# A Fourier-mixing and expert-lookup kernel: two token blocks row by row instead of one, and half of the table comparison moved into the score part

## Chip, cores and metric

The kernel runs on one core of one Trainium2 chip. The metric is the device time of one execution in microseconds (us), median of three runs; lower is better.

## What is computed

The reference, cut to what matters (S = 2048 tokens, D = 512, H = 32 heads, 64 keys per half, 4096 experts):

```
xn  = layernorm(x)
A   = dft_seq_re @ (xn @ dft_hid_re.T) - dft_seq_im @ (xn @ dft_hid_im.T)
q   = xn @ w_q                          # 32 heads, two halves of 128
s1, s2 = q1 @ k1.T, q2 @ k2.T           # 64 scores per half and head
top 2 of each half -> 4 pairs -> the best 2 experts per head, softmax g over them
act = gelu(xn . u[expert])              # 64 chosen rows of u per token
out = x + A + sum(g * act * v[expert])  # 64 chosen rows of v per token
```

## The kernel before, in words

The 2048 tokens are 16 blocks of 128. The work has three parts, one after the other on TensorE (PE).

- **Fourier part.** The input is normalized, folded by the symmetry of the cosine and sine tables, and multiplied; the result goes to `y_d` in device memory.
- **Score part.** A loop over 8 groups of heads (`j`, `NCH` = 8) and 16 token blocks (`i`): `scores` runs 12 matmuls for one block and group (L705), ScalarE (ACT) copies the result out of PSUM (L710), VectorE (DVE) finds the best keys (L713, L717). Around it ACT and GpSimd (POOL) split the query weights (`m_prep`, L158 to L166) and the tables u and v (`fill_uv`, L608 to L610) into pairs of 16-bit parts. `routing` turns the keys into expert numbers and softmax weights.
- **Expert part.** For 15 blocks (`NB = NT - NS`, `NS` = 1) the lookup is done as dense matmuls over all 4096 experts. `u_part` computes all dot products with u (L834) and a gelu on ACT (L837); `g_mm` builds from the expert numbers, with three DVE operations on 16-bit data (L860, L865, L868), the matrices whose product is the weight of each expert (L870); `w_part` multiplies weight and gelu and splits the product (L878, L882, L883); `v_part` multiplies with v (L890); `finish` adds and stores (L909). A loop over `b` runs `v_part` of block b in 8 steps, with `w_part` of the next block among them, and then `u_part` of block b + 2 in 8 steps, with `g_mm` among them.

The last block of tokens (`NS` = 1) does not go through the dense matmuls. `picked` gathers the 64 chosen rows of u and then the 64 of v for each token, one row per token at a time (`gather`, an indirect DMA issued by POOL, L914, 5 buffers `ga`). `dot` multiplies a row of u by the token and sums it on DVE (L943). `gate` does the gelu and the softmax weight of all 64 at once. `gain` scales a row of v on ACT (L954) and adds it to the output on POOL (L955). After each consumed row the next gather is issued. All dots come first, then all sums. These steps are dealt out evenly over "turns": there is one turn after each step of `v_part` (from b = 1) and of `u_part` (from b = 0 on, that is u of block 2), 16 (NB - 2) + 4 = 212 in all. `pick` orders the DVE and ACT instructions of a turn behind the matmuls of that step in the plan from which each engine's fixed instruction order comes (`follow`: an order, not a wait).

The kernel also verifies that its inputs have the symmetry it uses, and that the 16-bit scales fit. `compare(n)`, 64 of them, loads one 128x1024 piece of the cosine and sine tables, sums its first 128 columns (DVE, L989), subtracts or adds mirrored parts (DVE, L995 to L1029; for pieces 8 to 31 and 40 to 63 only L1008 and L1014, and for two in each eight a small extra), and sums what is left (ACT, L1030). `compare_w` does so for four pieces of the hidden table, `fit` sums absolute values on ACT (L1075, L1081). They are dealt out over the expert part by `step`. `verdict` combines the sums near the end. `add_x` loads the Fourier result for a block and adds x to it by a DMA that POOL issues (L903).

DMAs without another name are issued by SyncE (SP) in order. The tile framework gives out buffers and semaphores; each engine runs its instructions in the planned order.

Of the kernel before, what the change touches and what calls it, by code (L numbers as in the profile page):

```python
# [19 lines left out]
P = 128  # L20
# [12 lines left out]
NS = 1  # L33
# [3 lines left out]
def tile_fnet_peer(ctx, tc, x, ca, cb, c5, wt, wf, wr, wq, kt, ut, un, vn, out):  # L37
# [52 lines left out]
    NF = NW + 32 + NCH - 1  # L90
    sums_sb = cst.tile([P, 138 + NF + 3], F32, name="sums")
# [459 lines left out]
    def part_b(safe, stS, stP, stE, xt, u_sb, cmp_p):  # L551
# [146 lines left out]

        def scores(j, i, vals, idx):
# [3 lines left out]
            for kd in range(KD):  # L703
                for l, r in ((0, 0), (0, 1), (1, 0)):
                    nc.tensor.matmul(ps, xt[i][:, l, kd, :], m[:, r, kd, :], start=(n == 0),  # L705
                                     stop=(n == 3 * KD - 1))
                    n += 1
# [12 lines left out]
            return st[:, 512:]  # L720
# [29 lines left out]
        for (which, g), n in zip(fills, slots):  # L750
            todo[n].append(lambda at, w=which, g=g: fill_uv(w, g, at))
            todo[n - (3 if n < 113 else 1)].append(lambda at, w=which, g=g: fill_load(w, g))
        m_stage(1, wq_tile, 0)
        pend = None
        for j in range(NCH):
# [5 lines left out]
            for i in range(NT):  # L761
                spare = scores(j, i, vals, idx)
# [133 lines left out]
        def follow(i, after):  # L896
            tc.add_manual_dep(i, after.ins.name, mybir.DependencyInfo(
                mybir.DependencyClass.NoSync, mybir.DependencyReason.DATA), reason="pace")

# [12 lines left out]
        def gather(table, n, s):  # L912
            t = bp.tile([P, D], F32, tag="ga", name=f"ga{n}_{s}", bufs=5)
            nc.gpsimd.indirect_dma_start(  # L914
                out=t, out_offset=None, in_=table,
                in_offset=bass.IndirectOffsetOnAxis(ap=eix[:, n].rearrange("p k h -> p (k h)")[:, s:s + 1], axis=0))
            return t

        def picked(n):

            b = NB + n
            N = 2 * H
            G = {}
            T = {}

            def fetch(s):
                if s < 2 * N:
                    G[s] = gather((un, vr)[s // N], n, s % N)

            def begin():  # L930
                xs = T["x"] = bp.tile([P, D], F32, tag="xs", name=f"xs_{n}", bufs=1)
                o = T["o"] = bp.tile([P, D], F32, tag="ov", name=f"ov{n}", bufs=1)
                T["z"] = bp.tile([P, N], F32, tag="za", name=f"za{n}", bufs=1)
                nc.sync.dma_start(xs, x[b // 4, b % 4])
                nc.sync.dma_start(o, y_d[b])
                nc.gpsimd.dma_start(o, x[b // 4, b % 4], accum_op=ALU.add)
                for s in range(AHEAD):
                    fetch(s)
                norm(xs, xs, b)

            def dot(s):
                t = G.pop(s)
                nc.vector.scalar_tensor_tensor(t, t, 1.0, T["x"], op0=ALU.mult, op1=ALU.mult,  # L943
                                               accum_out=T["z"][:, s:s + 1])
                fetch(s + AHEAD)

            def gate():
                za = T["z"]
                nc.scalar.activation(za, za, AF.Gelu_apprx_tanh)
                nc.gpsimd.tensor_tensor(za, za, gts[:, n].rearrange("p k h -> p (k h)"), op=ALU.mult)  # L950

            def gain(s):
                t = G.pop(N + s)
                nc.scalar.activation(t, t, AF.Copy, scale=T["z"][:, s:s + 1])  # L954
                nc.gpsimd.tensor_tensor(T["o"], T["o"], t, op=ALU.add)  # L955
                fetch(N + s + AHEAD)

            return [begin, *(lambda s=s: dot(s) for s in range(N)), gate, *(lambda s=s: gain(s) for s in range(N)),
                    lambda: nc.sync.dma_start(out[b * P:(b + 1) * P], T["o"])]

        vr = vn.rearrange("c p d -> (c p) d")
        picks = [] if safe else [f for n in range(NS) for f in picked(n)]
        more = [range(1, 1 + max(0, n - k * (NB - 2) - 4)) for n, k in ((68, 5), (NF - NCH + 1, 4))]
# [13 lines left out]

        later = []

        def compare(n):  # L980

            ri, g, kk = n // 32, n // 8 % 4, n % 8
            odd = kk // 4
            t = bp.tile([P, 4, 4, 64], F32, tag="w", name=f"cx{n}", bufs=WB)
            tf = t.rearrange("p s q c -> p (s q c)")
            tv = t.rearrange("p s q c -> p s (q c)")
            nc.sync.dma_start(tf[:, :P], ca[ri, g, :, kk * P:(kk + 1) * P])
            nc.sync.dma_start(tf[:, P:], cb[ri, g, kk].rearrange("p b c -> p (b c)"))
            nc.vector.tensor_reduce(asum[:, n:n + 1], tf[:, :P], axis=AX.X, op=ALU.add,  # L989
                                    apply_absolute_value=True)  # L990
            sgn = (((1, 1, 1), (-1, 1, -1)), ((-1, -1, 1), (1, -1, -1)))[ri][odd]
            ops = [ALU.subtract if v > 0 else ALU.add for v in sgn]
# [131 lines left out]
        def step(it):  # L1124
            ready = later[:]
            del later[:]
            for f in ready:
                f()
# [209 lines left out]
```

## Time and profile before

| | |
|---|---|
| median of 3 runs | 1169.99 us (1169.89 to 1170.13) |
| profiled execution, its own time | 1171.21 us |
| profiled execution, span from first to last instruction | 1169.3 us |
| busy share of the span | PE 96%, DVE 84%, ACT 54%, POOL 42% |
| Fourier part, then score part | score matmuls start from 72.3 us to 443.4 us |
| expert part | first dense matmul at 446.6 us, last `v_part` matmul starts at 1162.4 us |
| rows of u gathered | 460.3 to 804.7 us (start of the issue) |
| rows of v gathered, summed | 812.2 to 1123.1 us, last sum starts at 1150.6 us |

In a row of the groups, a line number is followed by the engine, the operation, the tiles written and read, the shape and the count, then the busy time of all in us, the mean of one in ns, and the idle time of the engine just before them with what ended it. In a row of the table by stretches stand, after the stretch and its length, the busy time of each engine with the count of its instructions, the granted clock of PE, the share of the DMA engines and their GB/s. In a row of the timeline stand start and duration in us, engine, line and operation, and in brackets the idle time before it and what ended it.

### The profile page before, as it was taken

How to read it: one execution, taken by the hardware profiler on the slowest of the kernel's cores; microseconds unless marked ns; L12 is line 12 of the kernel's file. 1: busy time of each engine (PE TensorE's matmuls, PEld its weight loads, DVE VectorE, ACT ScalarE, POOL GpSimd, SP SyncE). 2: the span in 40 equal slices, each digit the busy share in tenths (PEclk: the TensorE clock that was granted, in tenths of full speed). 3: DMA queues.
4: the chain of work that ended last, by engine and by line, in shares of the span. 5: the costliest groups of instructions: out<-in, count | busy, mean ns of one | idle time of the engine just before them, and what ended most of it. 6: DMA issues, size and time to landing. Idle time of an engine off the chain costs nothing.

```text
span 1169.3 us, 29061 instructions
## 1 busy us (share of the span) xinstructions
PE 1118.0 (96%) x11681; PEld 734.0 (63%) x11681; DVE 987.5 (84%) x2946; ACT 632.3 (54%) x995; POOL 488.1 (42%) x411
## 2 busy tenths in 40 slices
PE   5799999999999999979999999999998999989997
PEld 4354555454454448939668578687685876858763
DVE  7878888798898997887998887988899689879895
ACT  2575546767767663443543534534546465464563
POOL 0021525548548342131343222323374666656742
PEclk9899999999999999989999999999999999999999
DMA  8254224132231113223554745645536456364554
GB/s 311 78 211 151 85 79 162 55 108 89 93 110 55 55 62 127 58 80 102 169 179 146 217 143 151 202 138 174 181 104 175 132 162 173 109 192 137 158 148 109
DMA packets 74369, 157.02 MB, mean 134 GB/s; under 512 B 10086, under 2 KB 26989, under 8 KB 74224
## 3 DMA queue, kind: packets, MB, share of 16 engines
q1 hardware_dynamic: 61522, 117.30, 30.1%
q0 software_dynamic: 12544, 37.76, 12.4%
q8 instruction: 93, 1.52, 0.5%
q14 instruction: 52, 0.43, 0.1%
q10 hardware_dynamic: 158, 0.01, 0.0%
HBM read 141.08 MB, written 13.96 MB: 133 GB/s over the span
## 4 chain that ended last, share of the span: by engine, by line
PE 71%; DVE 17%; DMA 4%; ACT 4%; issue 3%; SPq 0%; POOL 0%; DVEq 0%; ACTq 0%; POOLq 0%
PE s L705 27%; PE z L834 22%; PE v L890 14%; DVE L L860 3%; PE g L870 3%; DVE act L883 2%; DMA cx<-in_cb_dram 2%; DVE w L878 2%; ACT act L882 2%; DVE R L865 2%; PE m L144 2%; PE p L366 2%; DVE R L868 1%; DVE cx L1008 1%; DVE cx L997 1%
## 5 line engine op out<-in xcount | busy, mean ns | idle before, releaser
L834 PE MATMUL z<-xb,u 128*128 128x128 f16 x5760 | 335.1, 221 | 15.0 <-ACT act L837 12.6
L705 PE MATMUL s<-m,xq 128*128 128x512 f16 x1536 | 338.9, 379 | 0.0
L834 PEld LDWEIGHTS <-u 128*128 128x128 f16 x5760 | 327.6, 99 | 16.1 <-issue 13.3
L890 PE MATMUL v<-v,act 128*128 128x512 f16 x1440 | 319.7, 380 | 0.0
L705 PEld LDWEIGHTS <-xq 128*128 128x128 f16 x1536 | 148.4, 98 | 171.3 <-issue 0.2
L890 PEld LDWEIGHTS <-act 128*128 128x128 f16 x1440 | 138.2, 98 | 160.5 <-issue 1.9
L860 DVE TENSOR_TENSOR L<-io_lam,cmp 128x2048 f16<-128x2048 f16 x120 | 152.6, 1271 | 62.5 <-PE g L870 52.8
L837 ACT ACTIVATE act<-z,scl 128x512 f32<-128x512 f32 x120 | 81.9, 685 | 197.0 <-PE z L834 196.8
L914 POOL DMA_INDIRECT ga<-in_un_dram,eix x64 | 81.7, 1276 | 219.3 <-DVE ga L943 182.0
L713 DVE MAX8 vals<-ss 128x8 f32<-128x64 f32 x1024 | 152.6, 216 | 19.4 <-ACT ss L710 19.2
L955 POOL TENSOR_TENSOR ov<-ov,ga 128x512 f32<-128x512 f32 x64 | 98.3, 1535 | 114.0 <-ACT ga L954 112.4
L710 ACT ACTIVATE ss<-s,wsc 128x512 f32<-128x512 f32 x112 | 75.5, 680 | 81.8 <-PE s L705 71.7
L882 ACT ACTIVATE act<-w 128x1024 f16<-128x1024 f32 x60 | 79.5, 1351 | 54.5 <-DVE w L878 52.0
L717 DVE FIND_INDEX8 idx<-vals,ss 128x8 uint16<-128x256 f32 x256 | 107.1, 418 | 0.0
L914 POOL DMA_INDIRECT ga<-in_vn_dram,eix x64 | 89.2, 1393 | 34.7 <-DVE ga L943 17.3
L1030 ACT ACTIVATE cx<-cx 128x896 f32<-128x896 f32 x64 | 60.5, 946 | 67.4 <-DVE cx L1014 40.6
L883 DVE TENSOR_TENSOR act<-w,act 128x1024 f16<-128x1024 f32 x60 | 81.8, 1363 | 14.3 <-ACT act L882 14.1
L865 DVE TENSOR_TENSOR R<-io_c,cmp 128x512 f16<-128x512 f16 x120 | 81.5, 679 | 0.0
L878 DVE SCALAR_TENSOR_TENSOR w<-act,scl,g 128x1024 f32<-128x1024 f32 x60 | 75.4, 1276 | 2.2 <-PE g L870 1.8
L870 PEld LDWEIGHTS <-L 128*128 128x128 f16 x1920 | 56.4, 96 | 20.2 <-issue 8.0
L870 PE MATMUL g<-R,L 128*128 128x32 f16 x1920 | 58.6, 176 | 10.2 <-DVE R L868 7.8
L166 POOL TENSOR_TENSOR wq<-wq,wh 128x1024 f16<-128x1024 f32 x26 | 55.5, 2133 | 19.1 <-DMA wq<-in_wq_dram 16.4
(271 smaller groups left out, 1241.0 us busy)
## 6 DMA issues: line engine op xcount, KB each, us to landing
cx<-in_cb_dram SPq DMA_DIRECT2D x64, 448.0 KB, 4.4
wq<-in_wq_dram SPq DMA_DIRECT2D x32, 512.0 KB, 6.5
fit<-in_wq_dram SPq DMA_DIRECT2D x28, 512.0 KB, 5.4
uv<-in_ut_dram SPq DMA_DIRECT2D x16, 512.0 KB, 3.7
uv<-in_vn_dram SPq DMA_DIRECT2D x16, 512.0 KB, 3.7
xq<-in_x_dram SPq DMA_DIRECT2D x8, 512.0 KB
xt_d<-xq SPq DMA_DIRECT2D x16, 256.0 KB, 4.1
cx<-in_ca_dram SPq DMA_DIRECT2D x64, 64.0 KB, 2.5
```

The costliest lines, as they stand in the source:

```text
L705: nc.tensor.matmul(ps, xt[i][:, l, kd, :], m[:, r, kd, :], start=(n == 0), stop=(n == 3 * KD - 1))
L713: nc.vector.max(vals[:, i, w, :, h], s[:, g, :])
L717: nc.vector.max_index(idx[:, i, w].rearrange("p k h -> p (k h)"), vals[:, i, w, 0:2].rearrange("p k h -> p (k h)"), s[:, w * HC:g + 1, :]. ...
L834: mm = nc.tensor.matmul(p[:, cc * P:(cc + 1) * P], ug[:, l, c % 2, kd, :], xb[:, r, kd, :], start=(n == 0), stop=(n == 3 * KD - 1))
L860: nc.vector.tensor_tensor(L.rearrange("p t (l two) -> p t l two", two=2), io_lam.rearrange("p (l two) -> p l two", two=2).unsqueeze(1).to_ ...
L865: nc.vector.tensor_tensor(Rv, io_c.rearrange("p (c two) -> p c two", two=2).unsqueeze(1).to_broadcast([P, 16, NC // 2, 2]), bc(1, NC), op= ...
L870: nc.tensor.matmul(p[:, hf, t * NC:(t + 1) * NC], L[:, t, :], R[:, t, :], start=True, stop=True)
L878: nc.vector.scalar_tensor_tensor(w, act[:, :, ts], fw, p.rearrange("p h (n c) -> p c (h n)", c=NC), op0=ALU.mult, op1=ALU.mult)
L882: nc.scalar.activation(w16[..., 0], w, AF.Copy)
L883: nc.vector.tensor_tensor(w16[..., 1], w, w16[..., 0], op=ALU.subtract)
L890: mm = nc.tensor.matmul(pv, w16[:, c, :, l], vg[:, r, c % 2, :], start=(c == 0 and k == 0), stop=(c == NC - 1 and k == 2))
L914: nc.gpsimd.indirect_dma_start(out=t, out_offset=None, in_=table, in_offset=bass.IndirectOffsetOnAxis(ap=eix[:, n].rearrange("p k h -> p ( ...
```

## The change

`NS` becomes 2: 14 blocks go through the dense matmuls, two go row by row, 128 dots and 128 sums. Dots and sums alternate: the list `rows` takes one row of u and, 16 steps behind it, one row of v, and the gathers are issued in that order, still 5 ahead (`AHEAD`). The gelu and the weight are done for 16 dots at a time (`QG`), on ACT and POOL. There are 16 (14 - 2) + 4 = 196 turns for 256 such steps.

`compare` is moved up and takes 32 of its 64 pieces (`EARLY`: 8 to 23 and 40 to 55) in the score part, three and a quarter score tiles apart from tile 20 on. There its subtractions run on POOL in place of DVE, in a tag `cx` of its own with 2 buffers: the load four tiles ahead, the subtractions ordered behind the matmuls of tile n (`hold`), the sums on ACT two tiles later. For all 64, the sum of the first 128 columns moves from DVE to ACT. The 36 pieces that stay and the `fit` steps are dealt out evenly over the steps of `v_part` of blocks 1 to NB - 1 (`paced`).

```diff
-NS = 1
+NS = 2
...
+    EARLY = [*range(8, 24), *range(40, 56)]
+    early = cst.tile([P, 2, len(EARLY)], F32, name="early")
...
+        def hold(f, after):
+            made = nc.cur_bb.bb.instructions
+            first = len(made)
+            f()
+            for i in made[first:]:
+                if i.engine in (mybir.EngineType.DVE, mybir.EngineType.Activation, mybir.EngineType.Pool):
+                    follow(i, after)
...
+        def compare(n, at=None):
...
+            if at is None:
+                t = bp.tile([P, 4, 4, 64], F32, tag="w", name=f"cx{n}", bufs=WB)
+            else:
+                t = sp.tile([P, 4, 4, 64], F32, tag="cx", name=f"cx{n}", bufs=2)
+            v_eng = nc.vector if at is None else nc.gpsimd
...
-            nc.vector.tensor_reduce(asum[:, n:n + 1], tf[:, :P], axis=AX.X, op=ALU.add,
-                                    apply_absolute_value=True)
...
-                    nc.vector.tensor_tensor(v, v, tv[:, 0:1].to_broadcast([P, len(ix), 256]), op=o)
+                        v_eng.tensor_tensor(v, v, tv[:, 0:1].to_broadcast([P, len(ix), 256]), op=o)
...
+            def judge():
+                k = n if at is None else at
+                a, b = (chk, asum) if at is None else (early[:, 0], early[:, 1])
+                nc.scalar.activation(tf[:, P:], tf[:, P:], AF.Abs, accum_out=a[:, k:k + 1])
+                nc.scalar.activation(tf[:, :P], tf[:, :P], AF.Abs, accum_out=b[:, k:k + 1])
...
+        for k in range(len(EARLY)):
+            n = 20 + k * 13 // 4
+            checks.setdefault(n - 4, []).append(lambda mm, k=k: check_load(k))
+            checks.setdefault(n, []).append(lambda mm, k=k: hold(cx[k][0], mm))
+            checks.setdefault(n + 2, []).append(lambda mm, k=k: hold(cx[k][1], mm))
...
+        def fetch():
+            if rows:
+                k, n, s = rows.pop(0)
+                t = T[k, n, s] = bp.tile([P, D], F32, tag="ga", name=f"ga{k}{n}_{s}", bufs=AHEAD)
+                nc.gpsimd.indirect_dma_start(
+                    out=t, out_offset=None, in_=(un, vr)[k],
+                    in_offset=bass.IndirectOffsetOnAxis(ap=eix[:, n].rearrange("p k h -> p (k h)")[:, s:s + 1], axis=0))
+
+        def dot(n, s):
+            if s == 0:
...
+                T["z", n] = bp.tile([P, N], F32, tag="za", name=f"za{n}", bufs=2)
...
+            t = T.pop((0, n, s))
+            z = T["z", n]
+            nc.vector.scalar_tensor_tensor(t, t, 1.0, T["x"], op0=ALU.mult, op1=ALU.mult, accum_out=z[:, s:s + 1])
+            fetch()
+            if s % QG == QG - 1:
+                q = slice(s + 1 - QG, s + 1)
+                nc.scalar.activation(z[:, q], z[:, q], AF.Gelu_apprx_tanh)
+                nc.gpsimd.tensor_tensor(z[:, q], z[:, q], gts[:, n].rearrange("p k h -> p (k h)")[:, q], op=ALU.mult)
+
+        def gain(n, s):
+            b = NB + n
+            if s == 0:
+                T["o"] = o = bp.tile([P, D], F32, tag="ov", name=f"ov{n}", bufs=1)
+                nc.sync.dma_start(o, y_d[b])
+                nc.gpsimd.dma_start(o, x[b // 4, b % 4], accum_op=ALU.add)
+            o = T["o"]
+            t = T.pop((1, n, s))
+            nc.scalar.activation(t, t, AF.Copy, scale=T["z", n][:, s:s + 1])
+            nc.gpsimd.tensor_tensor(o, o, t, op=ALU.add)
+            fetch()
+            if s == N - 1:
+                nc.sync.dma_start(out[b * P:(b + 1) * P], o)
+
+        slots = [(n, s) for n in range(NS) for s in range(N)]
+        for i in range(len(slots) + QG):
+            rows += [(k, *slots[i - k * QG]) for k in range(2) if 0 <= i - k * QG < len(slots)]
+        picks = [] if safe else [lambda k=k, n=n, s=s: (dot, gain)[k](n, s) for k, n, s in rows]
...
+        todo_n = [n for n in range(68) if n not in EARLY]
+        units = [lambda n=n: (compare if n < 64 else compare_w)(n) for n in todo_n]
+        streams = [[fit_units, 0, 0], [units, 0, 0]]
...
+        def paced(k):
+            st = streams[k]
+            st[1] += 1
+            for f in st[0][st[2]:-(-len(st[0]) * st[1] // (4 * (NB - 2) + 2))]:
+                step(f)
+                st[2] += 1
...
-                if 0 < b < NB - 1 and (cg % 2 == 1 or cg == 6) or b + 1 == NB and cg < 4 or cg == 4 and b in more[0]:
-                    step(units)
-                if b and cg % 2 == 0 and (b + 1 < NB or cg < 4) or b + 1 == NB and cg in (1, 3) or (
-                        cg == 3 and b in more[1]):
-                    step(fit_units)
+                if 0 < b < NB - 1 or b + 1 == NB and cg < 4:
+                    paced(cg % 2)
```

More of the change, by code (lines that the diff above doesn't have):

```diff
@@ L910, in finish @@
             nc.sync.dma_start(out[b * P:(b + 1) * P], y)
[L912 to L919, printed above, removed]
-            b = NB + n
[L922 to L934, printed above, removed]
+        vr = vn.rearrange("c p d -> (c p) d")
@@ L947, in gate @@
[L947 to L959, printed above, removed]
```

146 lines of the change are left out of this document (77 added, 69 removed).

## Prediction

> **What bounds the kernel now.** First comes the table by stretches, to see which engine is full in which part: one stretch inside the score part, one of the expert part while rows of u are gathered and dotted, and one while rows of v are summed.
>
> ```profile
> 200.00:400.00 200.00, 200.00 (x1281) 97.21 (x1280) 178.12 (x954) 138.00 (x199) 113.74 (x106) 1.00 0.25 85
> 560.00:810.00 250.00, 248.34 (x3275) 184.56 (x3274) 215.60 (x419) 117.90 (x180) 76.34 (x59) 1.00 0.56 170
> 860.00:1110.00 250.00, 237.27 (x3132) 179.54 (x3130) 215.58 (x295) 133.57 (x207) 153.17 (x106) 0.98 0.52 152
> ```
>
> The columns after the length are PE, its weight loads, DVE, ACT, POOL. PE is full in the score part and in the dots stage. In the sums stage PE loses 12.7 us of 250, DVE is 86% busy as before, and POOL rises from 31% to 61%. How much a block of tokens takes in each stage is read from the DMA that POOL issues once per block, in its timeline:
>
> ```profile
> 564.78 1.02 POOL L903 DMA_DIRECT2D y<-in_x_dram  x1
> ...
> 791.86 1.01 POOL L903 DMA_DIRECT2D y<-in_x_dram  x1
> ...
> 887.98 1.01 POOL L903 DMA_DIRECT2D y<-in_x_dram  x1
> ...
> 1089.38 1.00 POOL L903 DMA_DIRECT2D y<-in_x_dram  x1
> ```
>
> Five blocks in the dots stage take 227.1 us, 45.4 us each; four in the sums stage take 201.4 us, 50.35 us each. PE does the same work in both. The groups of the two stretches show why the second is longer, first 560 to 810 us:
>
> ```profile
> L834 PE MATMUL z<-xb,u 128*128 128x128 f16 x2051 | 117.5, 219 | 1.4 <-ACT act L837 1.4
> L943 DVE SCALAR_TENSOR_TENSOR ga<-ga,xs 128x512 f32<-128x512 f32 x53 | 36.0, 685 | 0.0
> L865 DVE TENSOR_TENSOR R<-io_c,cmp 128x512 f16<-128x512 f16 x43 | 18.0, 419 | 0.0
> L868 DVE TENSOR_TENSOR R<-R,cmp 128x512 f16<-128x512 f16 x42 | 17.6, 420 | 0.5
> L943 DVE DVE_READ_ACCUMULATOR ga<-ga,xs 128x1 f32 x53 | 4.5, 85 | 0.0
> ```
>
> then 860 to 1110 us:
>
> ```profile
> L834 PE MATMUL z<-xb,u 128*128 128x128 f16 x1969 | 118.0, 224 | 10.6 <-ACT act L837 10.6
> L955 POOL TENSOR_TENSOR ov<-ov,ga 128x512 f32<-128x512 f32 x51 | 76.7, 1503 | 82.4 <-ACT ga L954 81.9
> L865 DVE TENSOR_TENSOR R<-io_c,cmp 128x512 f16<-128x512 f16 x42 | 44.7, 1064 | 0.0
> L1008 DVE TENSOR_TENSOR cx<-cx 128x512 f32<-128x512 f32 (+1 forms) x40 | 26.9, 715 | 3.5 <-DMA cx<-in_cb_dram 3.5
> L1030 ACT ACTIVATE cx<-cx 128x896 f32<-128x896 f32 x25 | 23.6, 946 | 27.9 <-DVE cx L1014 19.3 <-DVE cx L1022 4.1 <-DVE cx L1029 3.6
> L868 DVE TENSOR_TENSOR R<-R,cmp 128x512 f16<-128x512 f16 x42 | 22.1, 526 | 0.6
> L1014 DVE TENSOR_TENSOR cx<-cx 128x128 f32<-128x128 f32 (+2 forms) x30 | 9.3, 323 | 0.2
> L989 DVE TENSOR_REDUCE sums<-cx 128x1 f32<-128x128 f32 x25 | 7.0, 281 | 6.5 <-DMA cx<-in_ca_dram 6.5
> ```
>
> The same operation L865 takes 419 ns beside the gathers and 1064 ns beside POOL's sums, L868 420 and 526 ns. A sum on POOL and these DVE operations hinder each other, and the time for which the dots left DVE is eaten by it.
>
> **The change part by part.** *One block fewer in the dense matmuls.* The stretch in which rows are picked is bounded by these rows of the PE timeline:
>
> ```profile
> 526.83 13.56 PE L834 MATMUL z<-xb,u 128*128 128x128 f16 x240
> ...
> 1131.58 31.24 PE L890 MATMUL v<-v,act 128*128 128x512 f16 x144
> ```
>
> From u of the third block at 526.8 us to the end of the last v at 1162.8 us are 636.0 us: 13 blocks of u and v, and one v part alone (96 of the 144 matmuls, 20.8 us). So a block takes (636.0 - 20.8) / 13 = 47.3 us on the mean. After the change there are 12 such blocks and the v part: 12 P + 20.8 us, with P the time per block. At 47.3 us the kernel would gain 47 us. It breaks even at P = 51.3 us, with the score part's 2 us below at 51.1 us. All hangs on P.
>
> *POOL.* 256 steps over 196 turns are 128 / 196 x 16 = 10.45 pairs per block: a gather of u, a gather of v, a sum. The page has their means:
>
> ```profile
> L955 POOL TENSOR_TENSOR ov<-ov,ga 128x512 f32<-128x512 f32 x64 | 98.3, 1535 | 114.0 <-ACT ga L954 112.4 <-DMA cx<-in_ca_dram 1.1
> L914 POOL DMA_INDIRECT ga<-in_vn_dram,eix x64 | 89.2, 1393 | 34.7 <-DVE ga L943 17.3 <-POOL ov L955 16.0 <-DMA fit<-in_wq_dram 0.8
> L914 POOL DMA_INDIRECT ga<-in_un_dram,eix x64 | 81.7, 1276 | 219.3 <-DVE ga L943 182.0 <-DVE sums L989 15.1 <-PE z L834 9.1
> ```
>
> and its timeline the gaps between them and the two ends of their price:
>
> ```profile
> 463.14 0.95 POOL L914 DMA_INDIRECT ga<-in_un_dram,eix  x1 [0.30 <-issue]
> ...
> 831.26 0.32 POOL L950 TENSOR_TENSOR za<-za,gts 128x64 f32<-128x64 f32 x1 [2.75 <-ACT za L949]
> ...
> 909.82 1.28 POOL L955 TENSOR_TENSOR ov<-ov,ga 128x512 f32<-128x512 f32 x1
> 911.37 0.97 POOL L914 DMA_INDIRECT ga<-in_vn_dram,eix  x1 [0.27 <-POOL ov L955]
> 912.36 1.28 POOL L955 TENSOR_TENSOR ov<-ov,ga 128x512 f32<-128x512 f32 x1
> ...
> 956.55 1.28 POOL L955 TENSOR_TENSOR ov<-ov,ga 128x512 f32<-128x512 f32 x1
> 958.10 2.00 POOL L914 DMA_INDIRECT ga<-in_vn_dram,eix  x1 [0.27 <-POOL ov L955]
> 960.12 1.27 POOL L955 TENSOR_TENSOR ov<-ov,ga 128x512 f32<-128x512 f32 x1
> ```
>
> A sum with the gather behind it takes 2.54 us where DVE rests (909.82 to 912.36) and 3.57 us where DVE runs the 16-bit operations (956.55 to 960.12). A second gather adds at least 0.95 and a gap of 0.30 us. So a pair costs 3.79 us at the least; with all at their means 1.276 + 1.393 + 1.535 + 0.27 + 0.30 = 4.77 us. I take the means, for DVE will be no emptier than now (below). Then 10.45 x 4.77 = 49.9 us per block. L903 adds 1.0 us. The gelu and weight, once before, come eight times; POOL waited 2.75 us for ACT and took 0.32 us; eight of these over 12.25 blocks are 2.0 us per block, or nothing where the wait falls into another; I take 1.0. Between the two row-by-row blocks, `ov` has one buffer: SP's load waits for the store of the first, and POOL's own DMA and first sum wait behind it, with the gathers queued after; by the times to landing in the list of DMA issues,
>
> ```profile
> y<-in_x_dram POOLq DMA_DIRECT2D x15, 256.0 KB, 5.4
> out_dram<-y SPq DMA_DIRECT2D x15, 256.0 KB, 2.1
> ```
>
> at most about 10 us once (2.1 for the store, as much for the load, 5.4 for the DMA that adds x), at least nothing: 0.4 us per block. Together POOL needs 52.3 us per block, over the 50.35 us of the slower stage now, while PE's work fits into 45.4. POOL, 39% idle until now, becomes what sets the pace. DVE's dots and ACT's scales then wait for gathered rows, and what stands behind them in these engines' order waits with them, `g_mm` and the gelu of `u_part` included; PE loses the difference.
>
> *DVE.* In the sums stage it is busy 215.58 / 250 x 50.35 = 43.4 us per block. The dots bring 10.45 x (0.685 + 0.085) = 8.0 us. The 25 pieces compared in that stretch cost (26.9 + 9.3 + 7.0) / 25 = 1.73 us each, five per block; 36 over 13 blocks remain, so 2.2 fewer per block save 3.8 us, and the first sum of the others, 0.28 us each on ACT now, another 0.8. The sums come at 10.45 per block where now 51 in 250 us are 10.3, so their hindrance stays. DVE needs 46.8 us: below POOL, 93% of 50.35.
>
> *The score part.* These rows price it:
>
> ```profile
> L705 PE MATMUL s<-m,xq x1536: 376/379/390, 72.3 to 443.4; 128*128 128x512 f16 x192
> ...
> L663 POOL TENSOR_TENSOR if<-if,hoff 128x256 f32<-128x256 f32 x4 | 2.5, 612 | 2.2 <-DVE if L660 2.2
> L668 POOL TENSOR_TENSOR di<-if 128x128 f32<-128x128 f32 x4 | 1.8, 457 | 0.0
> L649 ACT ACTIVATE c<-c 128x64 f32<-128x64 f32 x4 | 1.0, 256 | 6.3 <-POOL c L646 6.3
> L1030 ACT ACTIVATION_READ_ACCUMULATOR cx<-cx 128x1 f32 x64 | 11.9, 186 | 0.0
> ```
>
> 128 tiles in 371 us are 2.9 us each, one piece per 9.5 us. On POOL it takes 1.28 + 0.61 + 0.46 = 2.35 us (512, 256 and 128 columns), 25% on top of 57%. On ACT it takes 0.946 + 0.186, and for 128 columns between 0.26 and 0.68, taken as 0.3, + 0.186: 1.6 us, 17% on top of 69%. Both fit, and the PSUM buffers for four score tiles cover some 9 us of lateness of ACT; without that cover each late sum would stop PE. SP's load waits for a free buffer of two, with the loads of weights and tables queued behind it. PE has no work less there, so nothing can be gained. I put 2 us, between 0 and 20.
>
> *The sum.* 12 x 52.3 + 20.8 = 648.4 against 636.0 us: +12.4, +2 for the score part: +14.4 us. On the profiled execution's 1171.21 us that is 1185.6; the median of the runs shown is 1.2 us lower, so 1184 us.
>
> [...] L865 is stretched by 0.64 us beside the sums, L868 by 0.11, and L1008, of the comparison, stays at 0.7 us. [...]
>
> **The rivals.** *POOL keeps up (ends faster).* If a pair costs under (51.1 - 2.4) / 10.45 = 4.66 us, only 0.11 us below the mean, POOL no longer decides at break-even, and P is what PE and DVE need, from 45.4 us (PE alone) to 50.35 us (the sums stage as it is). For it speaks the floor of 3.79 us; against it that the means, not the floors, add up, and that an engine in fixed order, which waits for dots and scales of others, is not busy to the last percent. With P at 49 us, nearer to the upper end as sums come throughout: 608.8 us, -27.2 + 2, 1145 us; the ends 1102 and 1161.
>
> *DVE sets the pace.* In the sums stage DVE waits 50.35 - 43.4 = 6.95 us per block, for PE, ACT and loads. If these waits stay and the dots come on top, P = 46.8 + 6.95 = 53.75 us: 665.8 us, 1202 us. The point from which it decides is 5.5 us of waits per block. If each dot were stretched like L865 by up to 0.64 us, DVE would be busy 46.8 + 6.7 = 53.5 us, the same price with no wait at all. Against it: fewer comparisons leave fewer waits for loads.
>
> *The score part gives way.* ACT at 86% and POOL at 82% come in lumps, and a sum on ACT that waits for POOL holds the eviction of the scores behind it. At 15 us above the forecast: about 1197 us.
>
> *The change doesn't do what it says.* If the planner leaves the early comparisons to late turns or bunches the steps, it acts like the second rival, and is counted there.
>
> **How the numbers follow.** The forecast gets 0.46, POOL keeping up 0.35, DVE 0.14, the score part 0.05. Under 0.2% (2.3 us), about what a measurement of this kernel can tell from no change, fall 0.04 of the forecast's lower end and 0.02 of the first rival's upper end. So faster 0.33, same 0.06, slower 0.61. Low is 1138 (P = 48.4 us), which leaves out 0.1 of the first rival; high is 1212 (P = 54.6 us), which leaves out 0.08 of the others. Both signs hold much; the likeliest case's own range is 1172 to 1197, P from 51.3 to 53.4 us.
>
> **What would show it.** Right: the issues of L903's successor stand 51 to 54 us apart throughout the picked stretch; POOL is over 90% busy with its gaps of 0.3 us counted; dots or scales wait for gathered rows; L865's successor takes about 1.06 us everywhere. Wrong: blocks of under 50 us with POOL waiting for ACT or DVE in the waits, or a pair that costs under 4.66 us. If the score matmuls end more than 5 us after 443.4 us, the score part was mis-sized.

## The result, and the profile after

The changed kernel takes 1230.06 us (median of 4 runs, 1224.31 to 1236.79) beside 1170.06 for the kernel before (1169.89 to 1170.48): ratio 1.0514, interval 1.0457 to 1.0572. It is slower, as forecast, but by 60 us instead of 14, and outside the range. Its profiled execution, the shortest of the four, took 1224.31 us with a span of 1222.5, so the spans differ by 53.2 us. The granted clock of PE fell from 0.986 to 0.962, but the matmuls themselves are no slower: the median is 379 ns for a score matmul and 219 ns for one of u in both traces.

Where these 53.2 us lie is read from three marks, as in the prediction: the start of the last score matmul, the start of u for the third block, and the end of the last v. First the tile list and the PE timeline of the changed kernel:

```profile
L787 PE MATMUL s<-m,xq x1536: 376/379/389, 70.1 to 447.6; 128*128 128x512 f16 x192
```

```profile
531.00 13.56 PE L929 MATMUL z<-xb,u 128*128 128x128 f16 x240
...
1168.38 20.46 PE L985 MATMUL v<-v,act 128*128 128x512 f16 x94 [0.31 <-DVE act L978]
```

- Up to u of the third block: 526.8 became 531.0 us, **+4.2**. All of it is there at the last score matmul (443.4 to 447.6). The first one came 2.2 us earlier than before (70.1 beside 72.3), so the score matmuls take 6.4 us longer.
- From there to the end of the last v: 636.0 became 657.8 us, **+21.8**, though one block fewer goes through it: P = (657.8 - 20.8) / 12 = 53.1 us.
- Behind the last v: before 1169.3 - 1162.8 = 6.5 us, now 1222.5 - 1188.8 = 33.7, **+27.2**.

The tail shows in POOL's timeline of the changed kernel, which ends with these lines (in brackets the idle time before the instruction and its releaser):

```profile
1185.78 0.41 POOL L1135 PARTITION_ALL_REDUCE fr<-fa  x1 [6.43 <-issue]
1186.37 1.19 POOL L1013 DMA_INDIRECT ga<-in_vn_dram,eix  x1 [0.19 <-POOL fr L1135]
1195.22 1.25 POOL L1045 TENSOR_TENSOR ov<-ov,ga 128x512 f32<-128x512 f32 x1 [7.66 <-issue]
1196.43 1.05 POOL L994 DMA_DIRECT2D y<-in_x_dram  x1
1197.22 1.56 POOL L1045 TENSOR_TENSOR ov<-ov,ga 128x512 f32<-128x512 f32 x1
1204.95 0.60 POOL L1136 PARTITION_ALL_REDUCE fr<-sums  x1 [6.17 <-issue]
1212.48 3.93 POOL L1045 TENSOR_TENSOR ov<-ov,ga 128x512 f32<-128x512 f32 x3 [6.92 <-issue]
```

`verdict` has two reductions over the partitions on POOL. They now stand among the last sums, and at each change between reduction and sum POOL does nothing for 6.2 to 7.7 us, without a releaser that the profile knows. The last dense block's `finish` on DVE waits for the DMA of L994, which stands in that queue (DVE's timeline):

```profile
1200.80 0.75 DVE L1000 SCALAR_TENSOR_TENSOR y<-v,scl,y 128x512 f32<-128x512 f32 x1 [18.44 <-DMA y<-in_x_dram]
```

The blocks themselves are read from the table by stretches and from the issues of L994, the successor of L903:

```profile
200.00:400.00 200.00, 194.68 (x1254) 94.63 (x1252) 168.47 (x905) 158.15 (x281) 162.03 (x172) 1.00 0.42 140
560.00:810.00 250.00, 224.34 (x2867) 163.60 (x2866) 230.17 (x332) 124.90 (x214) 206.28 (x150) 0.97 0.60 177
860.00:1110.00 250.00, 220.38 (x2809) 161.41 (x2807) 217.06 (x319) 123.70 (x211) 206.78 (x156) 0.95 0.59 178
```

```profile
576.04 0.98 POOL L994 DMA_DIRECT2D y<-in_x_dram  x1
...
1108.85 1.04 POOL L994 DMA_DIRECT2D y<-in_x_dram  x1
```

Ten blocks take 532.8 us, 53.3 each, in the first half of the stretch as in the second. PE, which was 99% and 95% busy, is 90% and 88% busy; POOL went from 31% and 61% to 83% in both. The groups of 560 to 1110 us:

```profile
L1045 POOL TENSOR_TENSOR ov<-ov,ga 128x512 f32<-128x512 f32 x105 | 149.9, 1427 | 13.8 <-ACT ga L1044 8.1 <-DMA ov<-in_x_dram 4.1
L1013 POOL DMA_INDIRECT ga<-in_un_dram,eix x106 | 144.6, 1365 | 38.3 <-POOL ov L1045 20.9 <-DVE ga L1029 10.8 <-issue 5.9
L1013 POOL DMA_INDIRECT ga<-in_vn_dram,eix x107 | 140.2, 1310 | 43.4 <-DVE ga L1029 15.8 <-issue 15.6 <-POOL ov L1045 5.7
L955 DVE TENSOR_TENSOR L<-io_lam,cmp 128x2048 f16<-128x2048 f16 x81 | 116.2, 1434 | 11.9 <-ACT cmp L697 7.9 <-PE g L965 3.9
L1029 DVE SCALAR_TENSOR_TENSOR ga<-ga,xs 128x512 f32<-128x512 f32 x109 | 93.5, 865 | 25.5 <-DMA ga<-in_un_dram,eix 25.4
L1044 ACT ACTIVATE ga<-ga,za 128x512 f32<-128x512 f32 x105 | 74.9, 714 | 132.9 <-DMA ga<-in_vn_dram,eix 105.9 <-POOL za L1034 14.8 <-DVE L L955 8.2
L960 DVE TENSOR_TENSOR R<-io_c,cmp 128x512 f16<-128x512 f16 x81 | 63.6, 785 | 0.0
L963 DVE TENSOR_TENSOR R<-R,cmp 128x512 f16<-128x512 f16 x81 | 49.5, 612 | 0.8
```

A pair costs 1.365 + 1.310 + 1.427 + 0.57 = 4.67 us; 10.45 pairs are 48.8 us, L994 and the weights bring it to about 50.7, and 2.6 us of waits in POOL's order remain. So POOL is occupied for some 95% of a block. DVE's operations are stretched too: L960 takes 785 ns and L963 612 (419 and 420 beside no sums), a dot 865 (685). By their time alone the two engines are close: DVE is busy for 90% of a block.

### The profile page after: what moved, and what is told of

Read it like the earlier page. It is cut to its first block, busy times and chain, and to the rows that moved or that the text cites. A ratio compares the mean times of both kernels' runs of the same rounds, so it can differ in the third digit from the quotient of the medians.

```text
span 1222.5 us, 28529 instructions
## 1 busy us (share of the span) xinstructions
PE 1089.9 (89%) x11070; PEld 703.2 (58%) x11070; DVE 1033.4 (85%) x2886; ACT 675.0 (55%) x1181; POOL 816.7 (67%) x706
## 4 chain that ended last, share of the span: by engine, by line
DVE 34%; POOL 20%; PE 20%; issue 11%; DMA 10%; ACT 5%; SPq 0%; POOLq 0%; DVEq 0%; ACTq 0%
PE s L787 8%; PE z L929 6%; DVE L L955 5%; POOL ga L1013 5%; POOL ov L1045 5%; DMA cx<-in_cb_dram 4%; DVE ga L1029 4%; DVE R L960 3%; POOL wq L168 3%; DVE vals L795 2%; DVE w L973 2%; POOL wq L167 2%; DVE act L978 2%; DVE idx L799 2%; DVE R L963 2%
## 5 line engine op out<-in xcount | busy, mean ns | idle before, releaser
L929 PE MATMUL z<-xb,u 128*128 128x128 f16 x5376 | 312.7, 220 | 26.3 <-ACT act L932 23.8
L929 PEld LDWEIGHTS <-u 128*128 128x128 f16 x5376 | 305.4, 98 | 28.3 <-issue 25.4
L1013 POOL DMA_INDIRECT ga<-in_un_dram,eix x128 | 169.3, 1323 | 78.5 <-DVE ga L1029 36.4
L1045 POOL TENSOR_TENSOR ov<-ov,ga 128x512 f32<-128x512 f32 x128 | 180.8, 1413 | 32.0 <-issue 14.6
L1013 POOL DMA_INDIRECT ga<-in_vn_dram,eix x128 | 165.1, 1290 | 51.3 <-DVE ga L1029 18.1
L955 DVE TENSOR_TENSOR L<-io_lam,cmp 128x2048 f16<-128x2048 f16 x112 | 161.0, 1438 | 22.3 <-PE g L965 13.6
L1044 ACT ACTIVATE ga<-ga,za 128x512 f32<-128x512 f32 x128 | 90.7, 714 | 153.6 <-DMA ga<-in_vn_dram,eix 122.1
L1029 DVE SCALAR_TENSOR_TENSOR ga<-ga,xs 128x512 f32<-128x512 f32 x128 | 107.9, 852 | 25.5 <-DMA ga<-in_un_dram,eix 25.4
L932 ACT ACTIVATE act<-z,scl 128x512 f32<-128x512 f32 x112 | 75.0, 679 | 70.5 <-PE z L929 68.1
L965 PEld LDWEIGHTS <-L 128*128 128x128 f16 x1792 | 53.3, 97 | 60.8 <-issue 49.3
L747 POOL TENSOR_TENSOR cx<-cx 128x512 f32<-128x512 f32 (+2 forms) x56 | 61.8, 1122 | 29.4 <-DMA cx<-in_cb_dram 23.0
```

Source lines behind the costliest of these rows:

```text
L929: mm = nc.tensor.matmul(p[:, cc * P:(cc + 1) * P], ug[:, l, c % 2, kd, :], xb[:, r, kd, :], start=(n == 0), stop=(n == 3 * KD - 1))
L955: nc.vector.tensor_tensor(L.rearrange("p t (l two) -> p t l two", two=2), io_lam.rearrange("p (l two) -> p l two", two=2).unsqueeze(1).to_ ...
L965: nc.tensor.matmul(p[:, hf, t * NC:(t + 1) * NC], L[:, t, :], R[:, t, :], start=True, stop=True)
L1013: nc.gpsimd.indirect_dma_start(out=t, out_offset=None, in_=(un, vr)[k], in_offset=bass.IndirectOffsetOnAxis(ap=eix[:, n].rearrange("p k h ...
L1044: nc.scalar.activation(t, t, AF.Copy, scale=T["z", n][:, s:s + 1])
L1045: nc.gpsimd.tensor_tensor(o, o, t, op=ALU.add)
```

## The experiments

The runs fall into five groups, each on a chip of its own beside the kernel before. On three chips (the first, second and fifth) the kernel before took 1169.7 to 1170.0 us, on two (the third and fourth) 1184.8 and 1180.1, and there the kernels with many gathers lose far more than it does; so times are compared on one chip. No chip served two of these groups, so what belongs to a chip and what to the hour can't be told apart. P is read from the issues of L994 (L903 in the kernel before). In the expectations A lays the loss on POOL, B takes the other side in the run at hand, C lays it on DVE (on the fifth chip: on the chain gather, scale, sum), D on the collision of POOL's sum with DVE's operations.

**First chip. The two reductions behind the last sum** (`follow` orders both behind POOL's last sum):

```
+follow(<each PARTITION_ALL_REDUCE of verdict>, <last POOL sum>)
```

> The changed kernel with one order changed: the two partition reductions of the verdict stand behind POOL's last sum in POOL's order, where they stood among the last sums. [...] Theory B (POOL is simply behind with its sums, and the reductions wait for data): the last sum ends at most 5 us earlier, 1225 us or more. [...]

1213.71 us, ratio 1.0362 (1.0334 to 1.0390). POOL's timeline has one change left:

```profile
1193.88 3.01 POOL L1045 TENSOR_TENSOR ov<-ov,ga 128x512 f32<-128x512 f32 x2
1202.69 0.41 POOL L1137 PARTITION_ALL_REDUCE fr<-fa  x1 [5.80 <-issue]
1203.02 0.68 POOL L1138 PARTITION_ALL_REDUCE fr<-sums  x1
```

The tail is 16.0 us instead of 33.7, near the 12.9 that remain of 33.7 without the last three of the changed kernel's four idle times (7.66, 6.17 and 6.92 us); theory B, with 1225 us or more, doesn't fit. The blocks are nearly as they were (P = 53.7 beside 53.3 us). The medians differ by 16 us; the profiled executions by 9.5 only, for in this one u of the third block came 2.9 us later and each block took some 0.4 us longer. So the place of the two reductions among the sums made two thirds of the added tail (17.7 of 27.2 us). Most of the rest is the one change that stays: it had been hidden under the last v and now stands behind it, and DVE's last `finish` waits in DVE's order behind the verdict, until 1205.4 us, 8.4 us after the last v.

**One block row by row, the rest as changed** (`NS = 2` back to `1`):

> The changed kernel with one block row by row in place of two (NS = 1): the early comparisons, the alternation of dots and sums and the pacing stay, 15 dense blocks. Theory A (POOL's load per block sets the pace): 4.8 pairs per block are 23 us of POOL per block, POOL no longer decides, blocks fall to 46 to 47.5 us; with 4 us more in the score part and no more than 10 us of tail, 1160 to 1172 us. Theory B (the early comparisons or the alternation are what slows the kernel): 1185 us or more.

1177.62 us, ratio 1.0062 (1.0042 to 1.0082). P is 46.65 us, inside theory A's range and near the prediction's 45.4 for PE alone: with 64 pairs over all turns POOL keeps up. The time lies between the two theories, for the tail has the same changes (POOL waits 7.10, 6.16 and 6.99 us with no releaser). So the interleaved order and the early comparisons alone do no harm to the blocks; the second block does.

**No early comparisons** (`EARLY = []`, all 64 on DVE in the expert part):

> The changed kernel with all 64 comparisons in the expert part, on DVE (two blocks row by row stay). DVE gets 32 x 1.73 us, 4.6 us per block, POOL's work per block stays. Theory A (POOL sets the pace): blocks stay at 53 to 54.5 us, the score part is 4 us shorter, 1225 to 1240 us. Theory C (DVE sets the pace): blocks grow by most of the 4.6 us, 57 to 58 us, 1265 to 1285 us.

1257.88 us, ratio 1.0756 (1.0727 to 1.0785). The time lies between the two expectations, but P, at 57.0 us, is what theory C gave (57 to 58) and not theory A (53 to 54.5). Of the 4.6 us that DVE gets per block (32 pieces of 1.73 us over 12 blocks), 3.7 come through, while POOL's busy time stays at 44 us per block. So POOL's queue alone does not set the pace: DVE has no slack beside it. The first u comes 4.5 us earlier, at 446.3 us; all in all the early comparisons help the change by some 28 us.

**The sums on DVE**:

```
-nc.scalar.activation(t, t, AF.Copy, scale=T["z", n][:, s:s + 1])
-nc.gpsimd.tensor_tensor(o, o, t, op=ALU.add)
+nc.vector.scalar_tensor_tensor(o, t, T["z", n][:, s:s + 1], o, op0=ALU.mult, op1=ALU.add)
```

> The changed kernel with the sums on DVE: one scalar_tensor_tensor for each row of v scales and adds, in place of the scale on ACT and the sum on POOL. POOL loses 10.45 x 1.7 us = 18 us per block and has only the gathers, DVE gains 10.45 x 0.69 = 7.2 us. Theory A (POOL's time and the collision of its sums with DVE set the pace): L back to 1.22, R to 0.42, dots to 0.69 us, which gives DVE about 9 us per block back; blocks of 46 to 49 us, 1130 to 1150 us. Theory C (DVE's own work sets the pace): 47.5 + 7.2 us, blocks of 53 to 55 us, 1205 to 1240 us with the shorter tail.

1141.13 us, ratio 0.9745 (0.9727 to 0.9763): on this chip faster than the kernel before, and inside theory A's range. Table and groups, 560 to 810 and 576 to 1062 us:

```profile
560.00:810.00 250.00, 239.95 (x3148) 176.31 (x3147) 226.16 (x416) 109.67 (x190) 169.70 (x118) 1.00 0.68 202
```

```profile
L955 DVE TENSOR_TENSOR L<-io_lam,cmp 128x2048 f16<-128x2048 f16 x80 | 97.7, 1221 | 9.9 <-PE g L965 7.0 <-ACT cmp L697 2.9
L1044 DVE SCALAR_TENSOR_TENSOR ov<-ga,za,ov 128x512 f32<-128x512 f32 x106 | 79.2, 747 | 16.2 <-DMA ga<-in_vn_dram,eix 9.4 <-issue 6.7
L1029 DVE SCALAR_TENSOR_TENSOR ga<-ga,xs 128x512 f32<-128x512 f32 x106 | 72.8, 686 | 8.8 <-DMA ga<-in_un_dram,eix 8.8
L963 DVE TENSOR_TENSOR R<-R,cmp 128x512 f16<-128x512 f16 x80 | 33.6, 420 | 0.4
L960 DVE TENSOR_TENSOR R<-io_c,cmp 128x512 f16<-128x512 f16 x80 | 33.4, 417 | 0.0
```

DVE takes on 10.45 x 0.747 = 7.8 us per block and is no fuller than before (226.16 against 230.17 of 250 us), since its other operations are back at 417 to 420, 686 and 1221 ns. PE rises from 90% to 96% and P falls to 48.6 us. With no sum on POOL one gap of this kind is left in the tail (6.61 us), and the last v covers it. The edit also takes the scale off ACT, so it shows what POOL's sums and the scale cost together: 4.7 us per block.

**Second chip. The sums on DVE, and behind each a useless third gather of 32 columns on POOL:**

> Sums on DVE as in e4, and in place of each sum on POOL a third, useless gather of 32 columns per row into a small buffer: POOL has about the same time per pair as in the changed kernel (3 x 1.7 us), but no elementwise operation. Theory A (POOL's time sets the pace): 10.45 x 5.1 + 1 us, blocks of 52 to 55 us, 1190 to 1215 us. Theory D (it is the collision of POOL's elementwise sums with DVE, not POOL's time): blocks of 48 to 50 us as in e4, 1140 to 1165 us.

1258.93 us, ratio 1.0732 (1.0670 to 1.0794), which answers nothing: nothing ordered the useless gathers, and the planner put 79 of the 128 into two blocks, which took 82 and 88 us; the later ones took 45 to 53. It shows that a crowded queue of gathers can stop the blocks, not what an evenly loaded one does. A paced repeat follows on the third chip.

**The changed kernel with both reductions last and without 32 of the 36 comparisons left in the expert part** (the four of `compare_w` stay, which the expectation overlooks; the missing sums are set to zero):

> e1 (the changed kernel with the reductions behind the last sum) without the 36 comparisons of the expert part that remain on DVE and ACT: that part of the check is left out. POOL's work stays. Theory A (POOL sets the pace): blocks of 51.5 to 53.5 us, 1190 to 1214 us. Theory C (DVE, with what the collisions add, sets the pace): DVE loses 5 to 7 us per block, blocks of 47 to 49.5 us, 1145 to 1170 us.

1184.91 us, ratio 1.0111 (1.0072 to 1.0151). Table, 576 to 1090 us:

```profile
576.00:1090.00 514.00, 469.63 (x6083) 347.26 (x6081) 435.73 (x570) 233.42 (x345) 425.03 (x331) 0.96 0.56 159
```

DVE falls to 85% busy, POOL stays at 83% (with its gaps 94%), and P falls from 53.7 to 51.5 us only, the lower end of theory A's range; the time is 5 us below that range and far above theory C's. DVE got 3.9 us per block back and 2.2 came through. So DVE alone doesn't set the pace, as POOL alone didn't without early comparisons: this run speaks for POOL, that one for DVE.

**The kernel before, its 64 sums on DVE** (L954 and L955 replaced as above):

> The kernel before with only its 64 sums moved from ACT and POOL to DVE. Theory D (the collision made the sums stage slower): L865's operation back from 1.06 to 0.42 us gives DVE back about as much as the sums cost it, PE no longer waits, blocks of the sums stage fall from 50.35 to 45.5 to 47.5 us, 1140 to 1152 us. Theory C (DVE's amount of work is what counts): DVE is no emptier, blocks stay near 50 us, 1165 to 1175 us.

1154.4 us, ratio 0.9861 (0.9823 to 0.9899), 2 us above theory D's range. P is 45.9 us on the mean, and 46.3 in the sums stage, where it was 50.35. L865 is back from 1064 to 421 ns there (groups of 860 to 1110 us):

```profile
L865 DVE TENSOR_TENSOR R<-io_c,cmp 128x512 f16<-128x512 f16 x44 | 18.5, 421 | 0.0
```

So it was POOL's sums that stretched DVE's operations in that stage, and with them (and ACT's scale) gone the stage is hardly longer than the dots stage was.

**One block row by row, early comparisons, sums on DVE:**

> e4 with one block row by row in place of two. With sums on DVE neither POOL nor DVE is near full: blocks of 45.5 to 46.5 us, 13 of them, 1150 to 1160 us. So the second block, which costs 60 us with sums on POOL, should be worth 10 to 18 us with sums on DVE. If the second block costs time in any form, this is below e4's 1141 us.

1161.73 us, ratio 0.9912 (0.9881 to 0.9944), P = 46.1. Beside the version with two blocks on the first chip the second block is worth about 20 us if the sums are on DVE (the two chips agree for the kernel before; 10 to 18 were expected); with the sums on POOL it cost 52 (1177.6 to 1230.1).

**Third chip. The third gather, paced** (ordered behind its row's sum on DVE):

> The kernel with the sums on VectorE, and behind each summed row a third, useless gather of 32 columns on GpSimd, now ordered behind that row's sum on VectorE, so that it comes once per pair as the GpSimd sum did. It puts back GpSimd's time per pair without an elementwise operation beside VectorE's. Theory A (GpSimd's queue alone sets the pace): a pair takes 1.37 + 1.52 + 1.17 and three gaps of 0.30, 4.96 us, or 4.6 if the two long gathers come back to 1.3 as they did where they were crowded; 10.45 pairs and 2.4 of other work make 50.5 to 54 us per block, 1165 to 1210 in all. Theory D (the GpSimd sum costs by slowing VectorE's own operations and by the chain gather, scale, sum, not by its time on the queue): 48.5 to 49.5 us per block, 1140 to 1155. VectorE's operations stay at 1.22, 0.42 and 0.69 us under both.

1367.06 us, ratio 1.1563 (1.1520 to 1.1606), P = 65.3: above all that either theory gave. The kernel without the third gather, on the same chip, says why this can't be read:

> The kernel with the sums on VectorE once more, beside the three others on one chip and for a narrower interval: 1138 to 1143, ratio to before 0.973 to 0.977, under every theory.

It is the kernel that took 1141.13 us, and it took 1218.16 here, ratio 1.0290 (1.0253 to 1.0326), P = 54.2. Two more runs left out all or half of its early comparisons:

> The kernel with the sums on VectorE and none of the 32 comparisons in the score part: all 64 on VectorE in the expert part. If the early comparisons pay there: score part 7 us shorter, VectorE's work 43.5 + 4.6 = 48.1 us per block, so blocks of 50.5 to 52 us against 48.6, sum +16 to +34: 1157 to 1175. If TensorE sets the pace of the blocks and VectorE has room: blocks stay within 1 us of 48.6, the 7 us of the score part come back, 1134 to 1146.

> As the one before it, with the first 16 of the 32 comparisons kept in the score part. Early comparisons pay: score part 3.5 us shorter, VectorE's work 45.8 us per block, blocks 49.3 to 50.3, 1146 to 1158. TensorE sets the pace: 1135 to 1143.

They took 1232.55 us without any and 1231.98 with half of them, so all 32 are worth 14 us here and the first 16 nothing that shows; their expectations, made for a chip like the first, missed.

The trace of the sums on DVE has here what none of the earlier ones has: PE stops in the middle of a group, in places after every 4 or 5 matmuls, and waits for nothing that the profile shows (PE timeline of e12_sums_dve_again):

```profile
816.22 3.01 PE L929 MATMUL z<-xb,u 128*128 128x128 f16 x51
819.53 0.38 PE L929 MATMUL z<-xb,u 128*128 128x128 f16 x4 [0.30 <-issue]
820.29 0.38 PE L929 MATMUL z<-xb,u 128*128 128x128 f16 x4 [0.38 <-issue]
821.04 0.44 PE L929 MATMUL z<-xb,u 128*128 128x128 f16 x5 [0.36 <-issue]
821.76 7.53 PE L929 MATMUL z<-xb,u 128*128 128x128 f16 x132 [0.28 <-issue]
```

**Fourth chip. Four kernels on one chip, for this condition:**

> The changed kernel itself once more. In the condition of its first measurement: 1224 to 1237, blocks of 53.3 us. If this call has the other condition, in which TensorE stalls between matmuls of a group: over 1245, and the trace has such stalls.

> The kernel before, for its trace beside the others: 1169 to 1171 without the stalls, 1179 to 1187 with them. If it is the gathers beside the matmuls that bring the stalls, this kernel with one block has a few, but less than half as many per block as the one with the sums on VectorE.

> The kernel with the sums on VectorE a third time: 1138 to 1143 and blocks of 48.6 us without the stalls, 1212 to 1223 and 54.3 with them.

> The kernel with the sums on VectorE and a useless third gather, ordered behind each row's sum. Without the stalls: theory A (GpSimd's time per pair alone) 50.5 to 54 us per block and 1165 to 1210; theory D (the GpSimd sum acts through VectorE's operations and the chain) 48.5 to 49.5 and 1140 to 1155. With the stalls: 65 us per block and 1356 to 1372 as before, which tells neither apart.

| kernel | us | ratio to before (interval) | P, us |
|---|---|---|---|
| before, again | 1179.33 | 0.9989 (0.9963 to 1.0016) | 48.1 |
| changed, again | 1246.73 | 1.0550 (1.0513 to 1.0586) | 55.0 |
| sums on DVE | 1203.79 | 1.0184 (1.0143 to 1.0224) | 52.9 |
| sums on DVE, paced third gather | 1349.52 | 1.1442 (1.1401 to 1.1482) | 65.4 |

The stalls are back, and the first three kernels are slower than on the chips without them (the fourth ran on none of those). The sums on DVE came out better than expected with stalls (1212 to 1223), the third gather too (1356 to 1372). PE's waits for nothing that shows (the waits list; us in total, times, longest): first the kernel before over eleven blocks, then the changed kernel over ten, the sums on DVE over ten, and the third gather over nine:

```profile
PE g L870 <- issue: 1.8, 5, 0.4
PE z L834 <- issue: 0.9, 4, 0.3
```

```profile
PE z L929 <- issue: 4.6, 18, 0.3
PE g L965 <- issue: 0.4, 1, 0.4
```

```profile
PE z L929 <- issue: 22.0, 67, 1.0
PE g L965 <- issue: 9.6, 23, 0.5
```

```profile
PE z L929 <- issue: 60.2, 135, 1.5
PE g L965 <- issue: 25.0, 45, 1.8
```

The same lists have no such line for the sums on DVE on the first chip, nor for the changed kernel as first measured, nor for the unpaced third gather on the second. With the sums on DVE the stalls grow with the gathers: 31.6 us in ten blocks of 21 gathers, 85.2 in nine blocks of 31; the kernel before, with 10, has 2.7. The third gather brings a sixteenth of the bytes of another one: per block the `software_dynamic` queue has 2169 packets and 5.96 MB with it, 1831 and 5.77 MB without (its lines in the queue lists of the two runs, over nine and ten blocks), which points to packets rather than bytes. But the number is not all: the changed kernel has 21 gathers per block as well and only 5.0 us, with a sum between them on POOL. POOL is busy for 389 of 589 us with the third gather; with its gaps it isn't full, while 85 of PE's 102 us of idle time are these stalls. So the test says nothing on A against D: the added gathers slowed PE, a third way that neither theory had. The expectation for the kernel before (less than half as many stalls per block) held.

**Fifth chip. The changed kernel without ACT's scale** (rows are summed unscaled):

> The changed kernel without ScalarE's scaling of the v rows (each row is summed unscaled), so GpSimd's sum waits for the gather alone. Theory A (GpSimd's own queue sets the pace): blocks stay within 1 us of the changed kernel's, 52.3 to 54.3 us without the stalls of TensorE or 54 to 56 with them; 1212 to 1237 or 1235 to 1255. Theory C (the chain sets it): the scale's 0.71 us and its wait fall out of 10.45 pairs, 4 to 8 us per block, 45 to 49.5 us, 1130 to 1185.

1470.53 us, ratio 1.2576 (1.2518 to 1.2635), P = 77.6, outside both. POOL's timeline:

```profile
807.56 0.96 POOL L1013 DMA_INDIRECT ga<-in_vn_dram,eix  x1 [0.30 <-issue]
811.98 1.27 POOL L1044 TENSOR_TENSOR ov<-ov,ga 128x512 f32<-128x512 f32 x1 [3.46 <-DMA ga<-in_vn_dram,eix]
813.65 0.97 POOL L1013 DMA_INDIRECT ga<-in_un_dram,eix  x1 [0.40 <-POOL ov L1044]
```

Without the scale the planner set each sum right behind the gather of its own row. In the changed kernel's order a sum stands one or two gathers of v later. Here POOL waits 2.5 us per pair for the landing on the mean (190.4 us for 76 sums), and all gathers behind it wait too. So the chain isn't tested, but the price of a wrong place in POOL's order is: 24 us per block.

**The kernel before with its sums on DVE, on the fifth chip:**

> The kernel before with its 64 sums on VectorE, again: 1150 to 1157, ratio 0.983 to 0.990 in the condition of its first run. If the stalls of TensorE come: they go with the number of gathers in a block, which this kernel has as the kernel before has, so 1160 to 1172 beside a kernel before of 1177 to 1187, the same ratio.

1153.19 us, ratio 0.9852 (0.9811 to 0.9894), P = 46.0. The first half of the expectation held. There are no stalls on this chip, so the second half wasn't put to the test: the version wasn't run where they occur.

## Why the prediction was right or wrong

**The failed step is the tail.** The sum ended at the last v and put nothing behind it. Of the 38.8 us between forecast and measured span change (53.2 - 14.4), 27.2 are there. What was overlooked is an order: `verdict` lies near the end, and two blocks of sums now reach to the last turn, so POOL's reductions and sums alternate. The trace of before had the price, hidden under the last v, in its single change from sum to reduction (POOL's timeline of the kernel before):

```profile
1157.98 0.41 POOL L1099 PARTITION_ALL_REDUCE fr<-fa  x1 [6.10 <-DVE sums L1098]
```

The releaser named there hid what it was: L1098 ended at 1157.1, so that line alone could not tell a wait for DVE from a price of the change. The runs tell them apart: the changed kernel pays 6.43 us at the first change, 7.66 at the change back, and 6.17 and 6.92 at the next two, with no instruction in that time and no releaser; with both reductions last it pays 5.80 once. What the runs show is the length of this time and that the order of the reductions decides how often it comes; what POOL does in it isn't shown.

**POOL's time per block came out near, a little low; that POOL alone sets the pace was not borne out.** Forecast 52.3 us, measured 53.1, which is 9.4 us over 12 blocks. The pair was put at 4.77 us and took 4.67; what was under-sized is what stands around the pairs: 1.4 us for weights and the `ov` switch, where 0.9 and 2.6 us of waits in POOL's order were measured. A pair thus cost what the first rival asked for (4.66 us), and the blocks came out no shorter all the same: the condition of that rival counted an engine in fixed order as free of waits, which its own second argument denied. The prediction let the fullest engine decide. The runs fit better with two engines in fixed order that wait for each other: 4.6 us more on DVE lengthened a block by 3.7, and 3.9 us less shortened it by 2.2.

**DVE was forecast at 46.8 us per block and took 47.7** (476.55 us in ten). The hindrance moved among the operations: L960 takes 785 ns, not the 1064 expected, but the dots take 865 and L955 1434 (685 and 1222 in the dots stage before). So the dots, which never ran beside sums in the trace of before, are stretched by 0.18 us each, not by the 0.64 of the second rival. The comparison is stretched too. The prediction read L1008 as unstretched at 0.7 us, but that mean mixed shapes; with shapes kept apart, first 560 to 810 us and then 860 to 1110 us of the kernel before, it went from 700 to 899 ns:

```profile
L1008 DVE TENSOR_TENSOR cx<-cx 128x512 f32<-128x512 f32 x10 | 7.0, 700 | 1.8 <-DMA cx<-in_cb_dram 1.8
...
L1008 DVE TENSOR_TENSOR cx<-cx 128x512 f32<-128x512 f32 x20 | 18.0, 899 | 2.2 <-DMA cx<-in_cb_dram 2.2
```

The second rival's P of 53.75 is as near to the measured one as the forecast; the run without 32 comparisons, which took DVE from 47.5 to 43.6 us per block and gained 2.2, speaks against DVE alone, and the run without early ones against POOL alone. How much of the 4.7 us between 53.3 and 48.6 that the sums cost is POOL's time and how much the stretching is open: both runs with a third gather and the one without the scale failed to tell them apart.

**The score part** was put at 2 us and took 4.2, inside its bounds of 0 to 20. ACT rose to 79%, POOL to 81% (86 and 82 were worked out); 2.2 us of the miss are here. The part itself grew by 6.4 us, and an earlier start gave 2.2 back. (The price of that rival should read 1199 us, 15 above the forecast, not 1197.)

**The range** (1138 to 1212) reached P = 54.6 but nothing for the tail; without the added tail the profiled run would have been at 1197. That is inside the range and still slower than before, so the sign didn't hang on the tail.

## What to carry over

Before a queue is filled to the last turn, look at what else stands in it near the end: a change between partition reduction and sum on GpSimd cost 6 to 8 us each time, and only cover had made it free. An elementwise sum on GpSimd can cost VectorE's other operations as much as it takes off VectorE: one operation of 0.75 us there in its place made the kernel before 1.4% faster on two chips, and the changed one faster both without the stalls (1230 to 1141 us) and with them (1247 to 1204). A gain of 2.5% on one chip became a loss of 2 to 3% on two others, so a kernel that leans on many gathers beside its matmuls is to be timed on more than one chip.

## What the runs showed of the hardware

- Near the end of the kernels with their sums on GpSimd, each change between a partition reduction and a sum took 5.8 to 7.7 us in which GpSimd ran nothing (5.79 us in the kernel before on the fourth chip, 7.66 in the changed kernel). In the changed kernel a gather directly behind a reduction started after 0.19 us, and with the sums on DVE (first chip) two reductions with only a DMA issue between them had such a time once: 6.61 us ahead of the first, none ahead of the second.
- Beside a stream of 128x512 sums on GpSimd, these operations of VectorE took longer: two 16-bit 128x512 operations 785 and 612 ns in the changed kernel and 1064 and 526 in the sums stage of the kernel before, instead of 419 and 420, a dot 865 (changed kernel) instead of 685, a 128x512 comparison 899 instead of 700 (kernel before). L973 did not: 1269 ns beside the sums (changed kernel) and 1276 without them (sums on DVE, first chip).
- TensorE's stalls, up to 1.9 us long (paced third gather, third chip) and in places after every 4 or 5 matmuls, came on two of the five chips, and with the sums on DVE they grew there with the gathers: 31.6 us in ten blocks of 21, 85.2 in nine blocks of 31. The profile's list of DMA queues for the sums on DVE (576 to 1062 us on the first chip, where it has no stalls) has a queue that it names instruction:

```profile
q8 instruction: 48, 0.79, 0.7%
```

That TensorE stalls because this queue is held up by the gathers' packets was a guess of the author's; the same list with stalls (588 to 1117 us on the fourth chip) speaks against it:

```profile
q8 instruction: 48, 0.79, 0.6%
```

As many packets took no longer: 0.7% of 16 engines over 486 us and 0.6% over 529 us are both about 1.1 us per packet. What stops TensorE, and why three chips are free of it, stays open.
